# A build-time order with a model of DMA rings, single tasks held or moved, and a two-tile sum, in a DeltaNet and feed-forward kernel

## The chip, the cores and the metric

The kernel runs on one core of a Trainium2 chip. A core has TensorE (PE; its weight loads are PEld in the profile), VectorE (DVE), ScalarE (ACT), GpSimd (POOL) and SyncE (SP), which here does nothing but issue DMA transfers. Each engine works through its own list of instructions, in the order in which the program wrote them, and waits at an instruction until what it needs is there. The metric is the device time of one execution in microseconds, the median of several runs.

## The reference

Queries, keys and values are 4 x 8 x 768 x 48 in fp32 (batch, heads, time steps, width), and beta is 4 x 8 x 768. The first half is a delta rule with a 48 x 48 state for each batch and head, the second half a feed-forward layer on its result:

```python
k_n = k / (np.linalg.norm(k, axis=-1, keepdims=True) + 1e-06)
for t in range(S):
    y[:, :, t] = np.einsum('bhd,bhde->bhe', q[:, :, t], state)
    v_old = np.einsum('bhde,bhd->bhe', state, kt)
    state = state + bt[:, :, :, None] * np.einsum('bhd,bhe->bhde', kt, vt - v_old)
...
x = attn_out.transpose(0, 2, 1, 3).reshape(B * S, H * D)      # 3072 x 384
h = x @ w_in                                                  # 3072 x 2048
g = h * np.cos(h)
out = g @ w_out                                               # 3072 x 384
```

The two weight matrices come as 64-bit floats. The kernel reads them as pairs of 32-bit words and makes 32-bit floats of them on the chip.

## The kernel before, in words

**The delta rule** is done in 24 units of 32 time steps, all batches and heads at once. Inside a unit the recurrence becomes a triangular system, and only the state goes from unit to unit. Two units make a pair, and 12 pairs make the 12 token blocks (256 tokens each) of the feed-forward part. The steps of unit n, with engine and line, are these.

- Loads of k, q and v (SP, L369, four DMAs each, one for each batch; from unit 8 on k takes eight).
- The key norms: square (ACT, L495), sum (DVE, L500), square root as a power (POOL, L512), and `scale` (DVE, L523 to L531: five instructions, of which the first, L523, adds 1e-6 to the norm). For the first four units these go unit by unit, afterwards by pairs. `weigh` (DVE, L548) scales v.
- `turn` (PE transposes, L560) and `turn_out` (ACT, L570) bring k and q into the layout for the products; from unit 8 on DVE does this (L576).
- `gram` (PE, L591, 128 small matmuls) forms key by key and key by query products; `gram_keys` (DVE, L602) and `gram_queries` (DVE, L611) scale and mask them. `gram_put` (SP, L629) writes the first to DRAM. For each pair `gram_get` (SP, L638) reads them back with one system in each partition.
- `inv` is the triangular inversion of a pair, 31 steps of a product and a difference, cut into seven tasks (L667 and L674). It starts from `eye` (ACT, L648). Pair 0 is inverted on DVE (the profile's `part_v`) and copied by `inv_out` (ACT, L678); all others are inverted on POOL. `put` (SP, L683) writes the inverse to DRAM (`z_dr`), `get` (SP, L692, four DMAs a unit) reads it back transposed (`zt`).
- `state` (PE, L709), `right` (DVE, L724), `solve` (PE, L740), `solve_out` (DVE, L750), `update` (PE, L763) and its sum into the state (DVE, L771), `within` (PE, L780), `within_out` (ACT, L791), `features` (PE, L799) and `features_out` (ACT, L807), which leaves the unit's rows of x.

**The weights** come in 28 tiles: 12 of w_in (512 KB each) and 16 of w_out (384 KB each). Each has a DMA (`weights`, SP, L460), a `split` (two on ACT, L468 and L470), a `shift` (two on DVE, L474 and L479) and an `add` (POOL, L483). The 28 DMAs are chained in order, and the tiles, the gated activations and the squares share eight buffers.

**The feed-forward part** of token block p: blocks 0 and 1 multiply by w_in plainly (`hidden`, PE, L820; the name carries block and group, so hidden 08 is group 8 of block 0, and a group is one `p_h` bank of 12 matmuls), later blocks with seven products in place of eight (`layer`, L936). The gate h cos h takes ACT (L860, L872, L873) and DVE (L865, L876). The output of block 0 is plain (`out`, L962; out 001 is its second task, each of four matmuls with their weights, named block, half, part), later blocks use a seven-product scheme (L1019) with sums on DVE. The result is stored by SP (L1080).

**What sets the order.** Nothing is ordered by hand: the class `Order` is a list scheduler that runs while the program is built. Each piece of work is a task with an engine, a cost, a due time, the tasks that it needs, the buffers that it makes and uses, and, for a transfer, the DMA time that it moves. Due times go backwards from the ends. `NUDGE` then shifts them by the kind of task, with one value for early units and one for later ones. `run` simulates the engines; whenever one is free it takes the ready task with the earliest due time, and writes its instructions. Two rules bend that for TensorE. `STICK` lets it stay with small or with large tiles for tasks whose due times are near, and `stall` models the fetch of its instructions in blocks of 256. A transfer is modelled by `IN_FLIGHT`: at most eight are on their way. What the simulation is told of costs (`add(...)` in `unit`, `inverse` and `weights`) thus decides only which order comes out; the engines then run that order at their own pace, and each waits at the first instruction whose inputs or buffers are not there.

Of the kernel before, what the change touches and what calls it, by code (L numbers as in the profile page):

```python
# [11 lines left out]
FP = mybir.dt.float32  # L12
I32 = mybir.dt.int32
U32 = mybir.dt.uint32
ALU = mybir.AluOpType
# [31 lines left out]
class Order:  # L47
# [9 lines left out]
    WINDOW = 818.445  # L57
    LAG = {"PE": 0.2, "DVE": 0.15, "ACT": 0.15, "POOL": 0.2, "SP": 2.0, "IN": 0.0}
    IN_FLIGHT, ISSUE = 8, 0.49
# [3 lines left out]
    STICK = 1.823  # L63
# [22 lines left out]
    def add(  # L86
        self, key, engine, cost, emit, deps=(), makes=(), uses=(), moves=0.0, due=1e9
    ):

        assert key not in self.tasks, key  # L90
        self.tasks[key] = [engine, cost, due, emit, set(deps), makes, uses, moves]
        for t in uses:
            self.users[t] = self.users.get(t, 0) + 1
        for tag, t in makes:
            self.tiles[t] = tag

    def count(self, key):
        if key == ("state", 0):
            return 0
        if key[0] == "layer":  # L100
            return 32 if key[3] in (1, 6, 7) else 16
        return self.COUNT[key[0]]

    def stall(self, key, now, commit):

        n = count = self.count(key)

        n = int(n * 1.034 if self.written < 1000 else n * 1.0054 + self.rest)
        cost, stall, there = self.tasks[key][1], 0.0, {}
        for i in range(self.written + 1, self.written + n + 1):  # L110
            t = now + cost * (i - self.written) / n + stall
            if (i + self.PHASE + self.AHEAD) % self.BLOCK == 0:
                there[(i + self.PHASE + self.AHEAD) // self.BLOCK + 1] = t + self.FETCH
            if (i + self.PHASE) % self.BLOCK == 0:
                block = (i + self.PHASE) // self.BLOCK
                stall += max(0.0, there.get(block, self.there.get(block, 0.0)) - t)
        if commit:
            if self.written >= 1000:
                self.rest += count * 1.0054 - n
            self.written += n  # L120
            self.there.update(there)
        return stall

    def run(self, wrote):
# [16 lines left out]
        for key, task in self.tasks.items():  # L141
            n = key[1] if len(key) > 1 and isinstance(key[1], int) else 0
            if key[0] in self.PAIRED:
                n *= 2
            task[2] += self.NUDGE.get((key[0], n < self.EARLY), 0.0)
# [1333 lines left out]
```

## Time and profile before

| | |
|---|---|
| median of 3 runs | 673.85 us (673.36 to 676.03) |
| the profiled execution | 673.89 us |
| its span, first to last instruction | 672.1 us |
| TensorE busy | 612.8 us (91%) |
| TensorE weight loads busy | 573.4 us (85%) |
| VectorE, ScalarE, GpSimd busy | 476.5, 295.7, 346.5 us |
| mean granted TensorE clock | 0.992 |
| first solve starts | 59.59 us |
| inversion of pair 0 on VectorE | 27.91 to 46.02 us |
| inversion of pair 1 on GpSimd | 37.74 to 77.83 us |
| last matmul ends | 667.07 us |

The profiled execution lies within 0.04 us of the median, so its parts can be used as they stand. Its time is 1.8 us more than the span. Two stretches must be told apart: up to about 60 us TensorE has little to do and waits for the first inverse, and after about 150 us it is busy nearly all of the time. A group of the profile is a line with an engine and a shape of tile; "idle before" is the time in which that engine stood still just before such an instruction, with what released it. SPq stands for SyncE's queue of DMA issues. In an answer in order of time the first column is the start, the second the duration (for a DMA issue the time to issue the whole group), and xN the number of instructions in a row.

### The profile page before, as it was taken

Reading aid. Unit: us, or ns where it says so; the run is one execution under the profiler, and the core shown is the slowest. Engines: PE = TensorE matmul, PEld = TensorE weight load, DVE = VectorE, ACT = ScalarE, POOL = GpSimd, SP = SyncE. Lnnn points to the kernel's source line nnn. Section 1 sums busy time; section 2 is a strip of 40 time slices with the busy share of each in tenths; the row PEclk is TensorE's granted clock in tenths of the full one; section 3 lists DMA queues with packets and bytes.
Section 4 is the critical chain, followed back from the end, with each engine's and each line's share of the span. In section 5 each row is a group of like instructions: output and inputs, shape, how many; then the busy total and the mean of one; then the engine's idle time right before and its main releaser. Section 6 shows DMA issues by size and latency. Waiting matters only on the chain.

```text
span 672.1 us, 27308 instructions
## 1 busy us (share of the span) xinstructions
PE 612.8 (91%) x11864; PEld 573.4 (85%) x11864; DVE 476.5 (71%) x911; ACT 295.7 (44%) x510; POOL 346.5 (52%) x734
## 2 busy tenths in 40 slices
PE   4303798999999999999999999999999999999996
PEld 3203786896999998999999999999999999999996
DVE  5799588978676785886876876776666656656661
ACT  4432457672153543653443444444434434434530
POOL 4369878976858328586285482582481670000000
PEclk9999798999999999999999999999999999999999
DMA  8897755455463453534524524515213202000000
GB/s 180 200 207 163 171 116 154 115 98 92 70 101 63 68 87 63 101 44 69 106 39 64 110 33 66 109 25 90 52 22 60 52 6 55 1 5 24 1 24 24
DMA packets 215516, 52.56 MB, mean 78 GB/s; under 512 B 206948, under 2 KB 210164, under 8 KB 215396
## 3 DMA queue, kind: packets, MB, share of 16 engines
q1 hardware_dynamic: 212964, 49.98, 38.7%
q8 instruction: 93, 1.52, 0.9%
q10 hardware_dynamic: 2176, 0.39, 0.4%
q0 software_dynamic: 256, 0.44, 0.3%
q14 instruction: 27, 0.22, 0.1%
HBM read 39.76 MB, written 11.01 MB: 76 GB/s over the span
## 4 chain that ended last, share of the span: by engine, by line
PE 83%; SPq 4%; DMA 4%; POOL 3%; issue 2%; DVE 2%; ACT 1%; ACTq 0%; POOLq 0%
PE p_h L936 29%; PE p_out L1019 28%; PE p_h L820 5%; PE p_kq L709 4%; PE p_out L962 3%; PE p_s L763 3%; PE p_u L740 3%; PE p_kq L780 3%; PE p_g L591 2%; PE p_o L1019 2%; SPq L369 1%; PE p_z L799 1%; SPq L692 1%; POOL knrm L512 1%; DMA zt<-z_dr 1%
## 5 line engine op out<-in xcount | busy, mean ns | idle before, releaser
L667 POOL TENSOR_TENSOR part<-z,gb 128x126 f32<-128x126 f32 (+22 forms) x341 | 132.3, 388 | 108.2 <-DMA gb<-g_dr 47.0
L674 POOL TENSOR_TENSOR z<-z,part 128x126 f32<-128x126 f32 (+22 forms) x341 | 139.9, 410 | 26.7
L936 PE MATMUL p_h<-x_ffn,w_in 128*128 128x128 f32 x1120 | 143.6, 276 | 0.1
L936 PEld LDWEIGHTS p_h<-x_ffn,w_in 128*128 128x128 f32 x1120 | 135.5, 192 | 1.4 <-issue 0.2
L1019 PE MATMUL p_out<-w_out,g_ffn 128*128 128x192 f32 x672 | 123.8, 329 | 0.1
L1019 PEld LDWEIGHTS p_out<-w_out,g_ffn 128*128 128x128 f32 x672 | 107.5, 190 | 1.2
L860 ACT ACTIVATE turns<-p_h 128x512 int32<-128x512 f32 x96 | 56.9, 595 | 101.0 <-DVE p_h L955 74.6
L1019 PE MATMUL p_out<-w_sum,g_ffn 128*128 128x192 f32 x496 | 91.5, 329 | 0.0
L872 ACT ACTIVATE turns<-turns 128x512 f32<-128x512 f32 x96 | 60.4, 629 | 45.1 <-DVE turns L865 44.9
L1019 PEld LDWEIGHTS p_out<-w_sum,g_ffn 128*128 128x128 f32 x496 | 79.3, 190 | 0.9
L876 DVE TENSOR_TENSOR g_ffn<-turns,p_h 128x512 f32<-128x512 f32 x96 | 65.4, 682 | 18.8 <-ACT turns L873 18.0
L865 DVE SCALAR_TENSOR_TENSOR turns<-p_h,turns 128x512 f32<-128x512 f32 x96 | 65.5, 684 | 16.3 <-ACT turns L860 16.0
L1035 DVE TENSOR_TENSOR g_ffn<-g_ffn 128x512 f32<-128x512 f32 x88 | 62.6, 712 | 13.6 <-PE p_out L1019 13.0
L512 POOL TENSOR_TENSOR knrm<-ksum,halves 128x16 f32<-128x16 f32 (+1 forms) x14 | 36.3, 2598 | 66.8 <-DVE ksum L500 66.8
L873 ACT ACTIVATE turns<-turns,halfpi 128x512 f32<-128x512 f32 x96 | 69.3, 722 | 3.1
L955 DVE TENSOR_TENSOR p_h<-g_ffn,p_h 128x512 f32<-128x512 f32 x60 | 41.7, 695 | 38.8 <-PE p_h L936 32.8
L952 ACT COPY g_ffn<-p_h 128x512 f32<-128x512 f32 x60 | 35.0, 583 | 74.8 <-PE p_h L936 74.6
L820 PE MATMUL p_h<-x_ffn,w_in 128*128 128x128 f32 x384 | 48.3, 284 | 0.4 <-issue 0.4
L820 PEld LDWEIGHTS p_h<-x_ffn,w_in 128*128 128x128 f32 x384 | 45.7, 198 | 1.8 <-issue 0.8
L1069 DVE SCALAR_TENSOR_TENSOR o<-p_out,o 128x192 f32<-128x192 f32 x74 | 25.2, 353 | 26.3 <-PE p_out L1019 25.5
L936 PE MATMUL p_h<-x_sum,in_sum 128*128 128x128 f32 x320 | 43.7, 280 | 0.0
L936 PEld LDWEIGHTS p_h<-x_sum,in_sum 128*128 128x128 f32 x320 | 39.5, 191 | 1.1
(94 smaller groups left out, 784.9 us busy)
## 6 DMA issues: line engine op xcount, KB each, us to landing
pairs<-in_moe_w_in_dram SPq DMA_DIRECT2D x12, 512.0 KB
gb<-g_dr SPq DMA_DIRECT2D x24, 256.0 KB
pairs<-in_moe_w_out_dram SPq DMA_DIRECT2D x16, 384.0 KB
vp<-in_v_dram SPq DMA_DIRECT2D x96, 48.0 KB
out_dram<-o SPq DMA_DIRECT2D x23, 192.0 KB
z_dr<-z SPq DMA_DIRECT2D x12, 256.0 KB
zt<-z_dr SPq DMA_DIRECT2D x96, 32.0 KB
kp<-in_k_dram SPq DMA_DIRECT2D x128, 24.0 KB
```

The costliest lines, as they stand in the source:

```text
L512: nc.gpsimd.tensor_tensor(out=scales[m][2][:, part], in0=sums[m, part.start][:, 0:n], in1=halves[:, 0:n], op=ALU.pow,)
L667: eng.tensor_tensor(out=part, in0=z[:, 0:rows, j, None].to_broadcast(shape), in1=a[:, j, None, j + 1 :].to_broadcast(shape), op=ALU.mult,)
L674: eng.tensor_tensor(out=behind, in0=behind, in1=part, op=ALU.subtract)
L820: nc.tensor.matmul(p_h[:, i], w_in[:, t, (4 * k + i) * 128 : (4 * k + i + 1) * 128], xts[p][:, t, unit * 128 : (unit + 1) * 128], start=(t ...
L860: nc.scalar.activation(turns[p, f], hidden_of(p, f), AF.Copy, scale=TURN)
L865: nc.vector.scalar_tensor_tensor(out=r, in0=hidden_of(p, f), scalar=TURN, in1=t, op0=ALU.mult, op1=ALU.subtract,)
L872: nc.scalar.activation(r, r, AF.Abs)
L873: nc.scalar.activation(r, r, AF.Sin, bias=halfpi, scale=-2.0 * math.pi)
L876: nc.vector.tensor_tensor(out=place(p, f), in0=step_of(rests.pop((p, f)), f), in1=step_of(hidden_of(p, f), f), op=ALU.mult,)
L936: nc.tensor.matmul(p_h[:, e], in_sum[:, odd_tile, 4 * s + e] if a == "s" else w_in[:, a, f * 128 : (f + 1) * 128], x_sums[p][:, unit] if b ...
L1019: nc.tensor.matmul(p_o, left(p, part, a)[:, e % 4], right(e, b), start=(e == 0), stop=(e == FT // 2 - 1), skip_group_check=True,)
L1035: nc.vector.tensor_tensor(out=left(p, s, to), in0=left(p, s, one), in1=left(p, s, two), op=op)
```

## The change

No matmul, no activation and no transfer is added or left out. Four things differ.

1. **The model of transfers** in `Order.run`. The limit of eight in flight goes. In its place each queue has a ring of 128 descriptors, with a count for each kind of transfer (`DESCRIPTORS`), and an issue is held back until its descriptors fit. The model of instruction fetches gets 1.5 us more up to 130 us of model time. Some costs are closer to measured lengths: `gram_get` 1.2 to 1.0 (its transfer 1.6 to 1.8), `scale` 1.2 to 1.1, `weigh` 1.0 to 1.1 and 1.35 to 1.5, `turn` 0.9 to 1.0, `solve`, `update` and `within` of later units 0.52 to 0.66, `features` 0.35 to 0.4, the weights' transfer 1.65 to 1.8, and its factor for w_out 0.8 to 0.78, `beta_home` 0.5 to 0.8. Due times shift with `W_OUT`, `LOADS`, `FIRST`, `STEP` and a shorter `NUDGE`.
2. **Single tasks.** `HOLD` gives four tasks an earliest model time: `gram_get` of pair 1, `add` of tile 3, `gram_keys` of unit 1 and the load of v 4. `ON_ACT` gives two transfers to ScalarE's queue: `gram_put` of unit 0 and the load of weights tile 18.
3. **The 1e-6 sum.** `scale`'s first instruction becomes a sum of two tiles, with a constant tile `tiny` that one more memset fills at the start.
4. **The order that comes out.** SyncE's list up to the first fetch of an inverse, with w for a weights tile, gput, gget, put and get as above, and the four transfers of a load as one entry:

```
before: w0 k2 q2 w1 k3 q3 w2 gput0 gput1 w3 gget0 gput2 w4 gput3 k4 q4 w5 gget1 k5 v0 w6 q5 v1 w7 k6 v2 w8 put0 q6 v3 w9 get0
after:  w0 k2 q2 w1 k3 q3 w2 gput1 w3 gget0 w4 gput2 gput3 k4 w5 q4 k5 w6 v0 gget1 q5 w7 k6 v1 q6 w8 k7 put0 q7 w9 v2 get0
```

`gram_put` of unit 0 stands in ScalarE's list behind the square of unit 2's keys, and weights tile 18 behind `features_out` of unit 1.

TensorE's list from the first solve on:

```
before: solve0 update0 within0 gram4 state1 features0 solve1 hidden00 turn5 hidden02 update1 within1 hidden04 gram5 state2 hidden06 features1 out000 solve2 hidden08 update2 within2 hidden010 hidden012 features2 state3 turn6 out001 solve3
after:  solve0 update0 within0 features0 state1 gram4 hidden00 solve1 hidden02 turn5 hidden04 update1 within1 gram5 state2 features1 out000 turn6 hidden06 hidden08 solve2 hidden010 update2 within2 hidden012 features2 out001 gram6 state3
```

On VectorE the shift of tile 1 and the sum of unit 3's squares move ahead of `gram_keys` of unit 1, the shift of tile 2 ahead of `gram_keys` of unit 2, and the shift of tile 3 ahead of the first inversion. On GpSimd the add of tile 1 moves ahead of the norms of unit 3, and adds of w_in and w_out stand between the parts of the inversion of pair 1 in another order. From there to the end the lists of both kernels are alike but for neighbours that change places; TensorE changes between small and large tiles 166 times in place of 172.

The core of the diff (the costs listed above are left out of it, and the old `NUDGE`, which had a value for nearly every kind of task):

```diff
@@ class Order: constants @@
-    WINDOW = 818.445
+    WINDOW = 832.069
     LAG = {"PE": 0.2, "DVE": 0.15, "ACT": 0.15, "POOL": 0.2, "SP": 2.0, "IN": 0.0}
-    IN_FLIGHT, ISSUE = 8, 0.49
+    RING, ISSUE = 128, 0.49
+    DESCRIPTORS = {
+        "weights": 8, "gram_put": 64, "gram_get": 4, "put": 128, "blocks": 32, "store": 8,
+        "store_left": 8, "store_right": 8,
+    }
...
-    STICK = 1.823
+    STICK = 1.267
...
+    EARLY, NUDGE = 6, {('features', False): -50.6, ('left', True): 40.0, ('solve', True): -42.0, ('turn', False): 18.7, ('within', True): -6.1, ('weigh', False): -47.8, ('within', False): -19.2, ('features', True): -15.5, ('gate', True): -31.7, ('layer_out', False): -12.4, ('sum', False): 24.3, ('layer', False): -1.8, ('add', True): -16.7, ('update', False): -6.1, ('solve', False): -32.9, ('state', False): -9.6, ('right', True): 34.9, ('hidden', True): 14.3, ('gram', False): -8.1, ('out', True): -13.0, ('collect', True): -13.1, ('out', False): 0.3, ('x_sum', False): -20.0, ('inv', True): 1.1, ('v', True): 15.4, ('gram_put', False): 23.6, ('left', False): 26.9}
+    ON_ACT = {('gram_put', 0): 1, ('weights', 18): 1}
+    HOLD = {('gram_get', 1): 35.16, ('add', 3): 48.72, ('gram_keys', 1): 18.48, ('v', 4): 72.13}
@@ Order.add @@
+        if key in self.ON_ACT:
+            assert moves
+            engine = "ACT"
@@ Order.descriptors, new @@
+    def descriptors(self, key):
+        n = self.DESCRIPTORS.get(key[0], 16)
+        if key[0] in ("k", "gram_put") and key[1] >= 8:
+            n //= 2
+        return n
@@ Order.stall @@
-                there[(i + self.PHASE + self.AHEAD) // self.BLOCK + 1] = t + self.FETCH
+                there[(i + self.PHASE + self.AHEAD) // self.BLOCK + 1] = (
+                    t + self.FETCH + (1.5 if t < self.STEADY else 0.0)
+                )
@@ Order.run @@
-            task[2] += self.NUDGE.get((key[0], n < self.EARLY), 0.0)
+            task[2] += self.NUDGE.get((key[0], n < self.EARLY), 0.0) + self.NUDGE.get(key, 0.0)
...
-        flights, dma_free, hot = [5.5] * 4 + [8.5] * 4, 8.0, 1e9
+        flights, accepted, hot = [(7.0, 8.0, 8, "SP")], {}, 1e9
...
-                able = [x for x in heap if x[0] <= limit and fits(x[2])]
+                able = [
+                    x for x in heap
+                    if x[0] <= limit and fits(x[2]) and self.HOLD.get(x[2], 0.0) <= now
+                ]
...
                     for _ in range(parts):
-                        end = max(end, flights[-self.IN_FLIGHT]) + self.ISSUE
-                        dma_free = max(dma_free, end + 0.5) + moves / parts
-                        flights.append(dma_free + 1.4)
-                    done = flights[-1]
+                        end = max(end, accepted.get(engine, 0.0))
+                        begin = max(flights[-1][1], end + 0.95)
+                        flights.append(
+                            (begin, begin + moves / parts, self.descriptors(key), engine)
+                        )
+                        accepted[engine], room = end + 0.3, self.RING
+                        for a, b, n, on in reversed(flights):
+                            if on != engine:
+                                continue
+                            if n > room:
+                                accepted[engine] = max(
+                                    accepted[engine], a + (b - a) * (n - room) / n
+                                )
+                                break
+                            room -= n
+                        end += self.ISSUE
+                    done = flights[-1][1] + 1.4
@@ the kernel @@
+    def queue(*key):
+        return nc.scalar if key in Order.ON_ACT else nc.sync
...
+    tiny = const.tile([128, 2, H], FP, name="tiny")
+    nc.vector.memset(tiny, 1e-6)
...
-        nc.sync.dma_start(out=words[t], in_=src)
+        queue("weights", t).dma_start(out=words[t], in_=src)
...
-        nc.vector.tensor_scalar_add(knrm, knrm, 1e-6)
+        nc.vector.tensor_tensor(out=knrm, in0=knrm, in1=tiny[:, 0:n], op=ALU.add)
...
-            nc.sync.dma_start(
+            queue("gram_put", n).dma_start(
                 out=g_dr[heads, bs].rearrange("h b j i -> (b j) h i"), in_=g[rows, heads]
             )
@@ the tasks @@
-    W_IN, W_OUT, LOADS = 24.824, 4.888, 290.255
+    W_IN, W_OUT, LOADS = 24.824, -43.991, 290.993
...
-    FIRST, STEP = 2.12, 3.854
+    FIRST, STEP = 2.668, 3.87
```

## The prediction

> **What bounds the kernel now.** I read the busy times by stretch first, then TensorE's waits, then the SP queue and VectorE in order of time. The stretches (columns after the length: PE, PEld, DVE, ACT, POOL busy with counts, granted clock, DMA share, GB/s):
>
> ```profile
> 0.00:59.60 59.60, 14.26 (x297) 11.48 (x298) 46.29 (x127) 21.82 (x39) 33.81 (x52) 1.00 0.88 191
> 59.60:79.40 19.80, 15.07 (x445) 13.30 (x446) 11.73 (x26) 6.87 (x13) 17.61 (x35) 0.83 0.70 157
> 79.40:150.60 71.20, 68.18 (x1394) 59.70 (x1393) 60.13 (x102) 47.32 (x89) 58.30 (x85) 0.98 0.55 127
> 150.60:672.10 521.50, 515.25 (x9733) 488.86 (x9731) 358.30 (x659) 219.71 (x372) 236.76 (x564) 1.00 0.32 56
> ```
>
> From 150.6 on TensorE is busy 515.25 of 521.5 us, and some 5 of the rest is the tail after the last matmul (667.07). The same work must be done after the change, so only the first 150 us can move the end. TensorE's waits (total, times, longest):
>
> ```profile
> PE p_u L740 <- DMA zt<-z_dr: 25.6, 3, 25.0
> ...
> PE p_kq L709 <- issue: 2.5, 1, 2.5
> ...
> PE p_t L560 <- issue: 1.5, 1, 1.5
> ```
>
> The 25 us is the first solve, which starts at 59.59. I call that moment S. Behind it lies this chain: gram_keys, put and gather through DRAM, first inversion on VectorE (27.91 to 46.02), copy on ScalarE (to 46.69), then SP's queue:
>
> ```profile
> 47.22 0.71 SPq L460 DMA_DIRECT2D pairs<-in_moe_w_in_dram  x1
> 48.03 0.39 SPq L683 DMA_DIRECT2D z_dr<-z  x1
> 48.51 4.25 SPq L369 DMA_DIRECT2D qp<-in_q_dram  x4
> 52.80 1.94 SPq L369 DMA_DIRECT2D vp<-in_v_dram  x4
> 54.83 0.39 SPq L460 DMA_DIRECT2D pairs<-in_moe_w_in_dram  x1
> 55.27 4.23 SPq L692 DMA_DIRECT2D zt<-z_dr  x8
> ```
>
> The inverse is ready at 46.69, but SP reaches its put at 48.03: the queue, at 0.49 us an issue, ends last. The first of the four issues behind the put takes 2.77 us alone, where others take 0.45[...]. Later, TensorE loses time here:
>
> ```profile
> 107.26 1.38 PE L709 MATMUL p_kq<-st,kq_t 48*32 48x48 f32 x128
> 109.49 0.66 PE L560 MATMUL p_t<-consts,kp 128*128 128x128 f32 x4 [0.86 <-ACT x_ffn L807]
> 111.64 0.66 PE L560 MATMUL p_t<-consts,qp 128*128 128x128 f32 x4 [1.49 <-issue]
> 112.14 4.44 PE L962 MATMUL p_out<-w_out,g_ffn 128*128 128x384 f32 x8
> ```
>
> Eight output matmuls take 4.44 us here and 2.75 elsewhere: 1.7 us lost to the clock, after 2.35 us of gaps.
>
> [...] 93 instruction packets of 16 KB on queue 8, and all three "issue" gaps (ending 70.61, 75.84, 111.64) stand at one position modulo 256 in TensorE's stream; from 70.61, when one block arrives, to 75.84, when the next does, are 5.2 us. [...] the hidden group at 74.04 takes 5.3 us, later ones 2.84. [...] L523 took 1.25 us instead of 0.17 when L483 had begun 0.06 us before it, L474 1.76 instead of 0.68. [...]
>
> **The change, part by part.**
>
> *A. Up to the first inversion.* The 1e-6 sum is the same instruction count. [...] the edit alone is worth 0; the bound is 1.08 us saved at the fourth scale (1.25 less 0.17) and 0.1 lost. But POOL's second add now stands before the fourth norm, so nothing on POOL reads beside that scale: 1.08 is won by order. Against it, VectorE gets the fourth shift (0.68 + 0.43, 1.0 with overlap) ahead of the inversion, not behind it. And gram_keys of unit 1 moves behind the second shift and the fourth sum: second split ends 17.04, shift 1.0 (2.3 if POOL's add at 17.60 blocks it), sum 0.54, keys 0.41: done at 19.1 to 20.4, not 16.81. Its put goes out at 19.2 to 20.5. From second put to gather it was 4.5 us (18.50 to 22.99) behind two puts and one weights tile; one put less is about 1.2, so gather at 22.5 to 23.8, and 4.9 more (22.99 to 27.91): 27.4 to 28.7. VectorE itself: fourth scale at 22.5, 1.0; two shifts 2.0; four gram products 1.65: 27.2. So the inversion starts near 28.0, as before (27.91).
>
> *B. The SP queue to the z put.* From the third weights tile (done 17.88) SP had 46 issues to the put; it now has 49 (one g put goes to ScalarE; two loads of four move ahead of it, k 7 and q 6, one behind it, v 2). Before: 22.5 us of issue, 7.6 of waiting (30.15 in all). The waiting now: 1.9 for gram_keys 1 (was 0.2); 0 at the fourth weights tile (its 2.00 us lost 1.55 behind two puts); 2.3 at the gather (1.8); about 2.2 where two g puts follow the gather and a weights tile directly, with k 4 behind them (1.5); 2.4 over the rest, as before. 24.0 + 8.8: the put at 50.7, 2.6 later. The inverse, ready at 46.7, no longer matters.
>
> *C. Put to solve.* 11.56 us before (48.03 to 59.59), and again nine issues between put and fetch. The weights tile now stands before v, not right before the fetch: some 0.4 less. S' = 50.7 + 11.2 = 61.9, 2.3 later.
>
> *D. S' to the first hidden group and second solve.* Before, S + 19.8 with gram 4, state 1, features 0, solve 1 and hidden. Now features 0 comes first and waits for ScalarE's copy (0.46 and its hand-over) until +7.1; 0.77; state 1, 2.4: +10.3. [...] a 2 us stall, where it was 2.54. Gram 1.1, hidden 5.3, solve 1.5: +20.2. Loss 0.4; if the fetch runs ahead of that wait, a gain of 1.3.
>
> *E. Weights and POOL.* Gram 4 now ends at S' + 13.3 = 75.2 (66.97 before). SP stands at its put until 75.8, and behind that put wait the next weights tile (13), v 4 and tile 14. Tile 13 lands 3.6 later, split 1.0, its shift behind solve_out: its add ends at 85. POOL's order holds one more add (1.4), the last quarter of inversion 1 (5.3) and two adds (2.0) before the first output: 93.9; then three adds (4.1): 98. TensorE from 82.1: hidden 2.85, turn 1.0, hidden 2.9, update 0.9, within 0.9, gram 0.8, state 1.35, features 0.5: 93.3. The output waits 0.6 and takes 2.75, turn 1.1: 97.8; two hidden groups of 2.9 from 98: 103.8. Before, that set (turn 6 for solve 2) stood at 100.1. So +3.7 in all at this point.
>
> *F. Given back.* Turn 6 no longer stands behind state 3, and before state 3 now come output and gram, so that block has 4.6 us and more: the 2.35 us of gaps and the 1.7 of clock should go: -4.05. TensorE changes between small and large tiles 166 times, not 172; 2.94 against 2.84 for the same hidden group puts a change at 0.1: -0.6.
>
> *G. Other orders.* The new due times shuffle neighbours to the end of the run, mostly by one or two places; the same matmuls, with TensorE as cover. The weights tile issued from ScalarE waits for a free buffer on ScalarE; its activations queue behind it, covered by several us. What the cover misses I put at +1.5, from 0 to 4.
>
> Sum: 3.7 - 4.05 - 0.6 + 1.5 = +0.6 on 673.89 (the profiled execution: span 672.1 and 1.8 around it; it agrees with the median, 673.85). That is 674.5.
>
> **The rivals.**
> 1. *Slower, through E.* The late z put and SP's stand at gram 4's put push weights and adds so late that TensorE waits longer for L483 than F gives back. For: POOL is busy 58 of 71 us in that stretch, and add 11 came just in time before. Against: filler exists. It decides once the adds slip some 3 us beyond 98. With S' 1.5 later, 3 more there and 1 us of half clock: 680.
> 2. *Faster.* The put isn't late: the waits at loads shrink with the smaller queue, put at 48.2, S' 59.4, D's fetch ahead. Then -0.2 - 1.3 + 0.5 - 4.05 - 0.6: about 668.3. Against: 49 issues cost 24.0 us by themselves.
> 3. *Nothing of it reaches the end*, because TensorE has other work: that is the forecast's band.
>
> **Numbers.** 0.5% is 3.4 us, about what a measurement of this kernel tells from no change. Forecast band (670.5 to 677.3): 0.47. Slower: 0.32. Faster: 0.21. Range 668 to 681: A to E each carry about 1.2 us, F up to 4.
>
> **What would show it.** z put near 50.7 and first solve near 62: B and C. First output's wait for L483: E. No gap near turn 6 and 2.75 us for the second output group: F. The fourth scale at 1.0 us: A. It would be wrong if SP's waits before the put fell below 6 us, or a new gap of over 3 us came anywhere after 104.

## The result, and the profile after

The changed kernel takes 674.52 us (median of 12 runs, 672.76 to 677.73), beside 673.85 us for the kernel before (12 runs, 672.44 to 677.87). The ratio is 1.0006, with a 95% interval from 0.9989 to 1.0023: no difference that a measurement of this kernel can tell. The forecast was 674.5 us, with a band of 670.5 to 677.3 us for no difference.

The profiled execution of the changed kernel took 676.72 us (span 674.9), 2.2 us over its median. Single executions of one program are several microseconds apart here (those of the kernel before lie between 668.70 and 678.89 us over all the comparisons below). One pair of traces therefore shows where time goes, but not to a microsecond what the change is worth. A place is trusted below when several traces with the same order show it. Line numbers of the changed kernel are 39 higher than before at the loads of q, k and v (L369 is now L408) and 41 higher from the loads of weights on (L740 is now L781). The profile lists each fp32 matmul of the program as two records, so a hidden group of twelve stands as x24, an output task of four as x8, and a gram product, which has 32 matmuls and not 128, as x64.

Busy times by stretch of the changed kernel, cut at its first solve, at the end of its first hidden group and where the fourth output task of block 0 ends (columns as before: length, busy time and count of PE, PEld, DVE, ACT, POOL, granted clock, DMA share, GB/s):

```profile
0.00:60.30 60.30, 14.44 (x296) 11.46 (x297) 45.70 (x132) 23.51 (x41) 29.86 (x45) 1.00 0.87 190
60.30:77.30 17.00, 13.79 (x383) 12.21 (x386) 9.88 (x21) 4.33 (x8) 15.28 (x27) 0.80 0.64 156
77.30:149.50 72.20, 68.54 (x1460) 60.18 (x1460) 60.48 (x104) 47.64 (x88) 63.03 (x100) 1.00 0.58 130
149.50:674.90 525.40, 515.72 (x9732) 490.33 (x9730) 359.41 (x658) 218.79 (x373) 240.02 (x564) 1.00 0.32 55
```

The last stretch holds the same work as before (515.72 us of TensorE beside 515.25) and is 3.9 us longer. The cut at 149.50 comes 1.1 us earlier than its counterpart, 150.60. TensorE's waits (total, times, longest):

```profile
PE p_u L781 <- DMA zt<-z_dr: 23.4, 2, 22.8
...
PE p_kq L750 <- issue: 4.3, 4, 1.6
...
PE p_h L861 <- POOL w_in L524: 1.0, 1, 1.0
```

The wait for the first inverse is still the longest. The waits for instructions at the state product grew from 2.5 us in one place to 4.3 us in four, and the longest other new wait behind the first solve is one of 1.0 us for an add of w_in on GpSimd. SyncE's queue from the put of the inverse to its fetch:

```profile
50.87 0.40 SPq L724 DMA_DIRECT2D z_dr<-z  x1
51.37 3.45 SPq L408 DMA_DIRECT2D qp<-in_q_dram  x4
54.91 0.39 SPq L501 DMA_DIRECT2D pairs<-in_moe_w_in_dram  x1
55.35 1.91 SPq L408 DMA_DIRECT2D vp<-in_v_dram  x4
57.31 1.93 SPq L733 DMA_DIRECT2D zt<-z_dr  x4
```

The put goes out at 50.87, 2.84 us later than before, the fetch at 57.31, 2.04 later, and the first solve starts at 60.32, only 0.73 later. TensorE in the first hidden group after the first output (hidden 06, two matmuls in; the line runs on through hidden 08), at the second output task, and at the state product of unit 5:

```profile
96.54 5.18 PE L861 MATMUL p_h<-x_ffn,w_in 128*128 128x128 f32 x44 [1.01 <-POOL w_in L524]
...
111.14 0.49 PE L840 MATMUL p_z<-consts,y 128*128 128x128 f32 x3
111.46 2.75 PE L1003 MATMUL p_out<-w_out,g_ffn 128*128 128x384 f32 x8
...
171.45 0.74 PE L750 MATMUL p_kq<-st,kq_t 48*32 48x48 f32 x56 [1.58 <-issue]
172.12 4.55 PE L1060 MATMUL p_out<-w_out,g_ffn 128*128 128x192 f32 x16
```

The place around 110 us, where the kernel before lost 2.35 us in gaps and 1.7 to the clock (granted 0.62 from 112.1 to 116.6 us), is clean (granted 1.00 from 111.5 to 114.3). A new one stands at 170: a stop of 1.58 us in the middle of the state product, and behind it sixteen records in 4.55 us, for which the next sixteen need 2.87 (the granted clock was 0.62 from 172.1 to 176.6 us, 1.00 before and after). A second stop, 1.48 us, is at 312.5.

### The profile page after: what moved, and what is told of

Same layout as the page of the kernel before. It is cut to its first block, busy times and chain, and to the rows that moved or that the text cites. A ratio compares the mean times of both kernels' runs of the same rounds, so it can differ in the third digit from the quotient of the medians.

```text
span 674.9 us, 27292 instructions
## 1 busy us (share of the span) xinstructions
PE 612.5 (91%) x11864; PEld 574.2 (85%) x11864; DVE 475.5 (70%) x912; ACT 294.3 (44%) x510; POOL 348.2 (52%) x734
## 4 chain that ended last, share of the span: by engine, by line
PE 83%; DMA 8%; POOL 4%; issue 2%; ACT 1%; DVE 1%; SPq 1%; POOLq 0%; ACTq 0%
PE p_h L977 29%; PE p_out L1060 29%; PE p_h L861 5%; PE p_kq L750 4%; DMA pairs<-in_moe_w_in_dram 3%; PE p_out L1003 3%; PE p_s L804 3%; PE p_u L781 2%; PE p_kq L821 2%; PE p_g L632 2%; PE p_o L1060 2%; POOL part L708 1%; POOL z L715 1%; DMA z_dr<-z 1%; PE p_z L840 1%
## 5 line engine op out<-in xcount | busy, mean ns | idle before, releaser
L708 POOL TENSOR_TENSOR part<-z,gb 128x126 f32<-128x126 f32 (+22 forms) x341 | 137.6, 404 | 100.1 <-DMA gb<-g_dr 44.0
L1060 PEld LDWEIGHTS p_out<-w_out,g_ffn 128*128 128x128 f32 x672 | 109.3, 192 | 2.1 <-issue 0.5
```

What stands on the lines that cost most here:

```text
L708: eng.tensor_tensor(out=part, in0=z[:, 0:rows, j, None].to_broadcast(shape), in1=a[:, j, None, j + 1 :].to_broadcast(shape), op=ALU.mult,)
L1060: nc.tensor.matmul(p_o, left(p, part, a)[:, e % 4], right(e, b), start=(e == 0), stop=(e == FT // 2 - 1), skip_group_check=True,)
```

## The experiments

Two questions followed. Are the new stops at 170 and 312 us what takes back the start's gain? And does the time of the first solve, with which the sum began, reach the end at all? In all the kernels below but the eighth, the scheduler is replaced by a fixed list of its tasks (the list that it wrote itself, with the edit shown), so that one engine's order can be edited and the others stay. (Where a task of another engine must move with it, the edit shows that too.) "Before" and "after" name the two kernels; the ratios are to the kernel before.

### 1 and 2. The new start with the old rest, and the reverse

```diff
 the list of tasks of every engine, cut behind output task 011 (about 153 us):
-  after ... | after ...
+  after ... | before ...     # the first kernel
+  before ... | after ...     # the second
```

> The changed kernel up to the second task of block 0's second output half (about 153 us), and from there every engine in the order of the kernel before. First theory: the new start gains 1.2 us by 150 us, and the new order behind it gives this back in two places where TensorE waits for its instructions in the middle of a state product (1.59 us at 169.9, with 1.7 us of half clock behind it, and 1.48 us at 312.5). Then this kernel has no such wait after 150 us and takes 672.6 us, 1.2 under the kernel before. Second theory: the start is what costs, the two waits belong to one execution, and the order of the rest is worth nothing: 674.5 us, as the changed kernel.

> The complement: the kernel before up to the same task, and from there the order of the changed kernel. First theory: both waits at the state products are there again, at about 171 and 314 us, and the time is 2 to 3.6 us over the kernel before, 676 to 677.5 us. Second theory: 673.9 us, as the kernel before.

The new start with the old rest took 675.67 us (ratio 1.0024, 1.0002 to 1.0045). The old start with the new rest took 673.45 us (1.0000, 0.9980 to 1.0020). The second one's trace has the stop again, at the state product of unit 5:

```profile
171.54 0.73 PE L709 MATMUL p_kq<-st,kq_t 48*32 48x48 f32 x55 [1.12 <-issue]
172.20 2.87 PE L1019 MATMUL p_out<-w_out,g_ffn 128*128 128x192 f32 x16
```

It has one at 310.7 us too, of 0.63 us. So the stops belong to the order and not to one execution, but they are shorter here (1.75 us together, not 3.06), and no half clock follows. The whole kernel is not slower for them. The first theory falls: it wanted 672.6 us for the first kernel and 676 to 677.5 for the second. In the first kernel's trace the old rest loses about as much in other places (0.50 us at 174.6, 0.74 in two stops near 246, 0.70 at 283.5). The new rest is worth nothing that these runs can tell. If either half costs something, it is the new start, by 1.6 us (0.1 to 3.0 by the interval), though the changed kernel, with the same start, is not measurably slower.

The start's gain, too, is found in one trace only. The fourth output task of block 0 ends at 149.5 us in the changed kernel, where the kernel before has 150.7. But it ends at 151.3 and 151.6 in the traces of kernels 1 and 3, which have the same start, and at 150.0 in kernel 2, which has the old one.

### 3. The state products moved away from the gram products

```diff
 TensorE, unit 5:
-  gram8 state5 out110 out111 solve5 out120
+  gram8 out110 out111 state5 out120 solve5
 TensorE, unit 11:
-  gram14 state11 out351 features10 layer417 solve11
+  gram14 out351 features10 layer417 state11 solve11
 VectorE:
-  turn_out9 right5
+  right5 turn_out9
```

> The changed kernel with two tasks moved on TensorE: the state product of unit 5 behind the next two output products (and its solve behind one more), and that of unit 11 behind an output product, the features and a layer step, so that no state product follows a gram product directly in these two places. First theory: the waits of 1.59 and 1.48 us go, with the half clock behind the first; 2 to 4 us less than the changed kernel, 671 to 672.5 us. Second theory: the time stays at 674.5 us, whether the waits are in the trace or not.

Measured: 681.33 us, ratio 1.0114 (1.0092 to 1.0136), the slowest of all. The trace shows what came instead of the two stops:

```profile
178.19 2.32 PE L1060 MATMUL p_out<-w_sum,g_ffn 128*128 128x192 f32 x8 [2.88 <-DVE o L1110]
...
320.65 0.59 PE L781 MATMUL p_u<-rhs,zt 32*32 32x48 f32 x40 [0.69 <-issue]
322.24 0.54 PE L781 MATMUL p_u<-rhs,zt 32*32 32x48 f32 x24 [1.00 <-issue]
```

At 178 the output product out 120 waits 2.88 us for VectorE to collect an earlier one. On VectorE that collecting stands behind `right` of unit 5, which needs the state product, and this now comes later. At 322 the stop for instructions (1.00 us) is back, 256 instructions further on, in the solve behind the state product. The 0.69 us at 320 stand at another place in a block, and their cause is open. Both theories miss: with the stops taken away at their places the kernel takes 6.8 us more than the changed one.

### 4. An earlier first solve: the put moved ahead

```diff
 SyncE:
-  q6 w8 k7 put0 q7 w9 v2 get0 w10 get1
+  q6 put0 w8 k7 q7 get0 w9 v2 w10 get1
```

> The changed kernel with SyncE's put of the first inverse moved ahead of weights tile 8 and the loads of k 7, and the first fetch of it moved ahead of weights tile 9 and v 2. The put goes out at 48.4 us (50.87 in the changed kernel), the first solve starts near 58.2 (60.32). If the adds on GpSimd decide how much of this arrives, the wait for L524 before the second hidden group after the first output grows from 1.0 to 3 us, and the whole time stays within 0.7 us of the changed kernel. If TensorE alone sets the pace up to 104 us, as the sum of the prediction had it for a change of the first solve, the time is 2 us less, 672.5 us.

The put went out at 48.80 and the first solve started at 57.29, 3.0 us earlier than in the changed kernel. The time was 675.6 us, ratio 1.0015 (0.9998 to 1.0032): not less.

```profile
64.87 1.56 PE L804 MATMUL p_s<-u,kp 64*64 64x96 f32 x32 [4.78 <-DVE knrm L564]
```

The gain is gone after one step. The first update waits 4.78 us and starts at 64.87, where the changed kernel has 63.80. It needs the scaled solution from VectorE, and there that stands behind the shift of tile 9, which comes late now:

```profile
62.54 0.69 DVE L515 SCALAR_TENSOR_TENSOR pairs<-pairs 128x512 uint32<-128x512 uint32 x1 [1.25 <-ACT pairs L511]
63.15 0.64 DVE L520 TENSOR_SCALAR w_in<-w_in 128x512 uint32<-128x512 uint32 x1
63.71 1.01 DVE L791 TENSOR_TENSOR u<-p_u,bz 128x384 f32<-128x384 f32 x2
```

The fetch was moved ahead of the load of tile 9, so the tile's split and shift are later, and VectorE goes through its list in order. (The view names L564, the short instruction right behind the scaled solution.) Neither expectation had named VectorE.

### 5. Step F alone, in the kernel before

```diff
 TensorE:
-  out000 solve2 hidden08 update2 within2 hidden010 hidden012 features2 state3 turn6 out001 solve3 hidden014
+  out000 turn6 hidden08 solve2 hidden010 update2 within2 hidden012 features2 state3 hidden014 out001 solve3
 ScalarE:
-  split17 cos06 ... split20 turn_out6
+  turn_out6 split17 cos06 ... split20
```

> The kernel before, with step F alone: on TensorE the transposes of unit 6 go ahead of hidden 08, hidden 10 behind the second unit's solve, and hidden 014 between the state product of unit 3 and the second output. If F was right by itself, the gaps of 0.86 and 1.49 us at 108.6 and 110.2 us go, the output behind them takes 2.75 us, and the end comes 2.3 us earlier, 4 with the half clock. The rival: the second output waits for an add of w_out on GpSimd (L483, done at 112.31 in the kernel before) whatever stands ahead of it, TensorE only waits elsewhere, and the whole time is within 1 us of the kernel before.

Measured: 673.81 us, ratio 0.9998 (0.9979 to 1.0016). The rival is right about the time and in that TensorE waits elsewhere. Its reason, the add on GpSimd, is not seen: the second output starts at 115.13 without a wait. The gaps around the transposes are gone, and others stand in their place:

```profile
110.51 0.28 PE L709 MATMUL p_kq<-st,kq_t 48*32 48x48 f32 x5 [1.78 <-issue]
110.72 4.57 PE L820 MATMUL p_h<-x_ffn,w_in 128*128 128x128 f32 x24
115.13 2.75 PE L962 MATMUL p_out<-w_out,g_ffn 128*128 128x384 f32 x8
...
119.92 0.85 PE L591 MATMUL p_g<-kq_t 48*32 48x64 f32 x64 [1.23 <-DVE u L750]
```

The stop for instructions moves from the transposes into the state product (1.78 us), the loss of speed falls on the hidden group (4.57 us for what takes 2.94), and the next gram product waits 1.23 us for VectorE.

### 6. The gather of pair 1 early again

```diff
 SyncE:
-  k4 w5 q4 k5 w6 v0 gget1 q5
+  k4 w5 gget1 q4 k5 w6 v0 q5
```

> The changed kernel with the gather for the inversion of pair 1 issued behind weights tile 5 instead of behind v 0, which undoes what the hold on it did. The inversion on GpSimd starts near 37.5 us (43.30), and the adds behind it come some 5 us earlier up to 90 us. If GpSimd sets the pace between 90 and 104 us, as step E had it, the wait of 1.0 us for the last w_in add at 95.5 goes and the end comes 1 us earlier. If TensorE has other reasons, nothing moves at 104 us but the wait.

The inversion on GpSimd started at 38.9 us, as meant. The time was 676.68 us, ratio 1.0043 (1.0022 to 1.0065). It is slower, and neither expectation had that. The put of the first inverse went out at 53.09 and the first solve started at 63.02, 2.7 us later. GpSimd, ahead at first, then waited for tiles (from 74.9 to 77.6 and from 81.1 to 83.5), had the second inverse ready at 92.1 instead of 90.4, and TensorE waited for that:

```profile
105.22 0.24 PE L781 MATMUL p_u<-rhs,zt 32*32 32x48 f32 x2 [1.52 <-DMA zt<-z_dr]
105.94 0.49 PE L781 MATMUL p_u<-rhs,zt 32*32 32x48 f32 x4 [0.48 <-DMA zt<-z_dr]
106.71 0.86 PE L781 MATMUL p_u<-rhs,zt 32*32 32x48 f32 x58 [0.29 <-DMA zt<-z_dr]
107.51 4.57 PE L861 MATMUL p_h<-x_ffn,w_in 128*128 128x128 f32 x24
```

So holding this one gather is worth about 2.5 us inside the new order (1.0043 beside 1.0006; the two intervals touch), though the inversion behind it begins 4.4 us later for it.

### 7. Everything early

```diff
 SyncE:
-  k4 w5 q4 k5 w6 v0 gget1 ... v1 q6 w8 k7 put0 q7 w9 v2 get0 w10 get1 v3
+  k4 w5 gget1 q4 k5 w6 v0 ... v1 w8 put0 q6 k7 get0 get1 w9 v2 v3 q7 w10
 VectorE:
-  in_sums30 shift9 solve_out0 scale(pair 2) shift10 update_out0 weigh1
+  solve_out0 in_sums30 update_out0 scale(pair 2) weigh1 shift9 shift10
 ScalarE:
-  split8 square(pair 3)
+  square(pair 3) split8
```

> The early gather, and with it the put of the first inverse ahead of q 6, its fetches ahead of weights tile 9, v 2, v 3 and q 7; on VectorE the first scaling of a solution ahead of the shift of tile 9, and that shift behind the second pair's weighing. Put at 47.6 us, first solve near 57.5, first update at 60.8 (63.80 in the changed kernel). If the first solve, the copy of its solution and GpSimd's adds together carry the start, TensorE is 3 us ahead at 104 us and the whole time is 3 us under the changed kernel, 671.5 us. If something else stands in between, its name will be at the longest new wait between 60 and 104 us.

First solve at 57.51 as expected, and 677.78 us, ratio 1.0058 (1.0040 to 1.0075).

```profile
63.14 1.56 PE L804 MATMUL p_s<-u,kp 64*64 64x96 f32 x32 [3.30 <-DVE u L791]
...
72.25 0.90 PE L840 MATMUL p_z<-consts,y 128*128 128x128 f32 x3 [6.12 <-ACT y L832]
```

The new wait has a name: 6.12 us for the copy of y on ScalarE (L832). ScalarE's order in time, same kernel:

```profile
63.90 0.67 ACT L509 ACTIVATE w_in<-pairs 128x512 f32<-128x512 f32 x1 [4.75 <-DMA pairs<-in_moe_w_in_dram]
...
70.62 0.66 ACT L509 ACTIVATE w_in<-pairs 128x512 f32<-128x512 f32 x1 [5.51 <-DMA pairs<-in_moe_w_in_dram]
71.19 0.64 ACT L511 ACTIVATE pairs<-pairs 128x512 uint32<-128x512 uint32 x1
71.73 0.46 ACT L832 COPY y<-p_kq 128x384 f32<-128x384 f32 x1
```

The copy stands behind the splits of tiles 9 and 10. Both wait for their tiles, 4.75 and 5.51 us, because those loads had been moved back.

### 8. The two-tile sum alone, in the kernel before

```diff
-        nc.vector.tensor_scalar_add(knrm, knrm, 1e-6)
+        nc.vector.tensor_tensor(out=knrm, in0=knrm, in1=tiny[:, 0:n], op=ALU.add)
```

> The kernel before with the 1e-6 sum as a sum of two tiles and nothing else. In the kernel before the fourth of these sums took 1.25 us with an add on GpSimd at work, others 0.17. If both forms wait for GpSimd alike, it takes 1.1 to 1.3 us here too. If the two-tile form runs freely beside it, 0.17, and the inversion starts up to 1 us earlier unless the gather from DRAM ends last.

One execution, 670.67 us, which decides nothing on the time. The sum itself is clear, VectorE first and GpSimd below:

```profile
22.23 1.24 DVE L525 TENSOR_TENSOR knrm<-knrm,tiny 128x8 f32<-128x8 f32 x1 [1.19 <-POOL knrm L514]
```
```profile
22.17 1.28 POOL L485 TENSOR_TENSOR w_in<-w_in,pairs 128x512 uint32<-128x512 uint32 x1
```

1.24 us beside an add on GpSimd that began 0.06 us earlier, exactly what the one-tile form took there. The third sum took 1.25 us beside another such add; the first two took 0.17 us, where GpSimd did nothing. In the changed kernel, where the add stands elsewhere, the fourth sum takes 0.17. The edit by itself shortens nothing here, and the order is what frees the sum, as step A had it.

### 9. A later put

```diff
 SyncE:
-  k7 put0 q7 w9 v2 get0
+  k7 q7 put0 w9 v2 get0
```

> The changed kernel with SyncE's put of the first inverse behind the load of q 7 instead of ahead of it: the put near 52.8 us (50.87), its fetch when it has landed, the first solve near 62.8 us (60.32). This is step B and C with the sign that the prediction gave them. If a later first solve goes through to the end, the time is 2 to 2.5 us over the changed kernel, some 0.4% over the kernel before. If the work behind it (adds, copies on ScalarE, VectorE) gives TensorE cover, as it did for an earlier solve, the time is within 0.7 us of the changed kernel.

```profile
53.89 0.40 SPq L724 DMA_DIRECT2D z_dr<-z  x1
...
57.65 2.29 SPq L733 DMA_DIRECT2D zt<-z_dr  x4
```

The put is 3.0 us later than in the changed kernel, but the fetch leaves at 57.65, just 0.34 later, and the first solve starts at 60.98, 0.66 later. 674.76 us, ratio 1.0010 (0.9994 to 1.0026). The put has landed within 3.8 us. In this trace the issues ahead of the fetch set it, and it hardly matters on which side of the put they stand. The expectation of 62.8 us for the solve was wrong, and the time within 0.7 us right.

### 10. The start arranged again

```diff
 SyncE:
-  k4 w5 q4 k5 w6 v0 gget1 ... v1 q6 w8 k7 put0 q7 w9 v2 get0 w10 get1 v3
+  k4 w5 gget1 q4 k5 w6 v0 ... v1 w8 put0 w9 q6 k7 get0 get1 w10 v2 v3 q7
 ScalarE:
-  split8 square(pair 3) split9 split10 within_out0 split11 features_out0
+  split8 split9 square(pair 3) within_out0 features_out0 split10 split11
 VectorE:
-  sum(pair 3) beta_home in_sums30 shift9 solve_out0 scale(pair 2) shift10 update_out0 weigh1
+  beta_home solve_out0 in_sums30 update_out0 shift9 scale(pair 2) sum(pair 3) weigh1 shift10
 GpSimd:
-  add12 add7 add8 add13 add9 inv16 add14 add15 add16 add10 add11
+  add7 add8 add9 inv16 add12 add13 add10 add11 add14 add15 add16
```

> The start of the changed kernel arranged again with every wait that the earlier first solve met taken out of its way: SyncE issues the gather for pair 1 behind weights tile 5, the put of the first inverse behind tile 8, tile 9 right behind it, then q 6, k 7 and the fetches; ScalarE makes the split of tile 10 behind the first copy of features; VectorE makes the first scaled solution ahead of the shift of tile 9; GpSimd adds tiles 7 to 11 ahead of those of w_out. First solve near 57.5 us (60.32), first update near 61 (63.80), state product of unit 1 near 65 (67.86). If the chain from the first solve is what the first 100 us wait for, the end comes 2.5 to 3 us earlier than in the changed kernel, 671.5 us. If the instruction blocks take it back (the gap ahead of the product of unit 4 grows from 0.64 to 3 us), or the weight tiles do, the whole time stays within 1 us of the changed kernel.

The start goes as meant: first solve 57.49, first update 61.27, state product 65.69, first hidden group 69.05 (71.90 in the changed kernel). But the time is 677.6 us, ratio 1.0060 (1.0036 to 1.0084; the trace is of the fastest of its five runs, 674.01 us).

```profile
85.19 0.89 PE L804 MATMUL p_s<-u,kp 64*64 64x96 f32 x32 [1.46 <-ACT kq_t L611]
...
89.70 0.80 PE L632 MATMUL p_g<-kq_t 48*32 48x64 f32 x60 [2.80 <-DVE st L812]
...
93.06 5.25 PE L1003 MATMUL p_out<-w_out,g_ffn 128*128 128x384 f32 x8
```

TensorE's lead of 2.85 us at 69 is gone by 93 us, where the first output now starts 3 us after that of the changed kernel (90.09): VectorE and ScalarE, whose work was pushed behind the first solve, are late around the second one.

### 11. The weights tile away from the fetch, in the kernel before

```diff
 SyncE:
-  put0 q6 v3 w9 get0 get1
+  put0 q6 w9 v3 get0 get1
```

> The kernel before with one thing moved on SyncE: weights tile 9 goes ahead of the load of v 3 and so no longer stands right before the fetch of the first inverse. The fetch is issued at the same time (55.27 to 56.26 in four traces of this start). If a 512 KB tile right ahead is what made the way from fetch to first solve 4.07 to 4.32 us there, it is 3.0 to 3.4 us here, as in the changed kernel, where four loads stand between, and the first solve starts near 58.7 us. If the length belongs to something else in the old start, it stays at 4.1 to 4.3. In either case the whole time stays within 0.7 us of the kernel before, since an earlier first solve met other waits in three runs.

```profile
53.71 0.39 SPq L460 DMA_DIRECT2D pairs<-in_moe_w_in_dram  x1
54.15 1.91 SPq L369 DMA_DIRECT2D vp<-in_v_dram  x4
56.10 4.83 SPq L692 DMA_DIRECT2D zt<-z_dr  x8
```

First solve at 59.83, so 3.73 us from fetch to solve. That lies between the two forecasts: in this one execution the tile explains about half of the difference. 675.48 us, ratio 1.0021 (0.9994 to 1.0049).

### 12. The first gram put back on SyncE

```diff
-    ON_ACT = {('gram_put', 0): 1, ('weights', 18): 1}
+    ON_ACT = {('weights', 18): 1}
 SyncE:
-  w2 gput1 w3
+  w2 gput0 gput1 w3
```

> The changed kernel with the first put of gram products back on SyncE, ahead of the second, as in the kernel before; weights tile 18 stays on ScalarE. If issuing it elsewhere saved the time of one issue alone, SyncE reaches the fetch of the first inverse 0.4 to 0.5 us later (57.3 to 57.8 in the traces of this start), and the whole time does not change beyond 0.7 us. If the put on its own queue also kept the others short, the gather of pair 0 and the fetch come 1 us or more later.

```profile
31.50 0.40 SPq L501 DMA_DIRECT2D pairs<-in_moe_w_in_dram  x1
...
52.67 0.41 SPq L724 DMA_DIRECT2D z_dr<-z  x1
...
57.47 2.74 SPq L408 DMA_DIRECT2D vp<-in_v_dram  x4
60.25 1.94 SPq L733 DMA_DIRECT2D zt<-z_dr  x4
```

The fetch left at 60.25, 2.5 to 2.9 us later than in the three traces with this start unaltered (57.31, 57.78, 57.41), more than the one issue accounts for. The gather of pair 0 did not move (22.90 beside 22.76 to 23.02), and SyncE came to weights tile 5 at 31.50, inside the range of those three traces (30.90 to 31.67). The time was lost after that, in loads that SyncE issued more slowly up to the fetch (the last four ahead of it took 2.74 us instead of 1.91). The delay of the fetch is thus seen in one execution, and how the put would cause it is not shown. And yet the time is 673.89 us, ratio 1.0002 (0.9983 to 1.0022).

## Why the prediction was right

The time was right, and so was the forecast that the difference would be too small to measure. The sign says nothing: +0.6 us was forecast and +0.7 measured, well inside the noise. Neither of the two signs of being wrong came: SyncE's waits before the put are 8.9 us by the count of step B, and the longest new gap after 104 us is 1.58 us. Of the steps some were right and some wrong, and the runs show that the first of them do not carry the result. That the number came so close is luck.

**A, up to the first inversion.** The value of the edit alone (nothing) was the author's estimate, and the eighth kernel shows it; of the two examples that the prediction gave, L474 is another operation (scalar_tensor_tensor), and kernel 8 shows the sum of two tiles itself. The fourth scale took 1.02 us, as said. gram_keys of unit 1 at 19.42, its put at 20.32 and the gather at 22.76 lie in the ranges given. The inversion started at 29.00, not 28.0; in the other traces with this start at 28.75 to 29.47, with the old one at 27.52 to 28.98. The gather took longer to land than the 4.9 us taken from before. Nothing waits for it: the inverse is ready at about 47.7, and SyncE reaches its put at 50.87.

**B, SyncE's queue.** Right: 50.7 said, 50.87 measured (51.36 and 51.03 in the other two traces).

**C, put to solve.** Wrong by 1.7 us: 11.2 said, 9.45 measured. The failing term is "some 0.4 less": it is about right for the weights tile that no longer stands right before the fetch, but it was taken for all that changes between put and solve. From fetch to solve it was 4.07 to 4.32 us in four traces with the tile right ahead, 3.01 to 3.37 with four loads between, 2.01 to 2.48 with the tile six or more microseconds ahead. Kernels 9 and 12, where the tile stands 3.3 and 3.5 us ahead with four loads between, have 3.33 and 2.41. The eleventh kernel, which moves the tile alone, gives 3.73: so the tile is worth 0.3 to 0.6 us by itself. What makes up the rest, no run takes apart. Besides, the first issue of loads behind the put held the queue for 1.97 us, not 2.77.

**D, to the fourth gram product.** Said S + 13.3, measured S + 11.65. The stop for instructions was 0.64 us, not 2. The 2 was the author's estimate, from the 5.2 us between the ends of two stops before. Those 5.2 us are no constant: in the kernel before, whole blocks of 256 instructions are worked off in 2.98 us (at 168.2) and in 1.87 us (at 190.0) without a stop behind them.

**E, weights and GpSimd.** The mechanism is there in the hidden group behind the first output (1.01 us of waiting for L524 at 96.54); the 0.6 us at that output itself did not come, and the size is not as said. First output at 90.09, not 93.9; hidden 08 done at 101.72, not 103.8. Against the step's own comparison, 100.1 before, the kernel is 1.6 us later there, not 3.7, and C's and D's misses, 3.2 us together at the end of the fourth gram product, more than account for the difference. A further 1.4 us went in the solve behind it, which takes 2.27 us instead of 0.88 (0.54 of it waiting for its fetched inverse). No step had that.

**F, given back.** The place is clean and the output takes 2.75 us, as said. From the end of the second pair's solve to the end of the second output, this pair of traces has 10.29 us after and 14.34 before for the same work (one hidden group, the transposes and the state product, which are elsewhere after, taken out): 4.05 us, as said. As the value of an order it was wrong. The old start was without the 1.7 us of half clock by itself in the second kernel (2.75 us for the same output), and step F done alone gained nothing (the fifth).

**G, the rest.** +1.5 said (0 to 4). In the pair of traces it is more, 3.9 us after the fourth output task, by two stops and the half clock behind one. Over many runs the new rest costs 0.0 us (0.9980 to 1.0020 with the old start). The 0.6 us for fewer changes of tile were not tried. And the opening of the prediction, that only the first 150 us can move the end, is wrong: kernel 3 changes the order behind 165 us alone and takes 6.8 us more than the changed kernel.

**The sum.** By the steps, the first solve's delay went 1:1 into the end until something gave it back. This is the assumption that the runs take away. Four kernels with the changed kernel's order on TensorE, and with the gather of pair 1 held, differ in the first solve by 5.4 us and in nothing that can be measured at the end:

| kernel | put | fetch | first solve | ratio to before |
|---|---|---|---|---|
| 4, put first | 48.80 | 55.28 | 57.29 | 1.0015 (0.9998 to 1.0032) |
| the changed kernel | 50.87 | 57.31 | 60.32 | 1.0006 (0.9989 to 1.0023) |
| 9, put later | 53.89 | 57.65 | 60.98 | 1.0010 (0.9994 to 1.0026) |
| 12, put on SyncE | 52.67 | 60.25 | 62.66 | 1.0002 (0.9983 to 1.0022) |

Passed on 1:1, the ratio of kernel 4 would lie 0.0045 below that of the changed kernel and that of kernel 12 0.0035 above it; they lie 0.0009 above and 0.0004 below. An earlier solve meets VectorE (kernel 4), ScalarE (7) or both at the second unit (10). Where a later one is made good is not shown. In kernel 12 the wait for the w_in add at about 98 us is 0.72 us instead of 1.01, and the first output takes 2.75 us, not 3.25; but against the changed kernel's trace the delay is still 2.4 us at the fourth output task (151.9 beside 149.5), and against those of kernels 1 and 3 (151.3 and 151.6) little of it is left. The third rival, "nothing of it reaches the end, because TensorE has other work", describes the result better than the sum that gave the number, though it is not TensorE alone that has the other work. In the pair of traces the terms are about +3.0, -4.0 and +3.9; over many runs the last is nothing, and step F, tried alone, gains nothing. The number came out right because terms of opposite sign, too large for what the runs show, nearly cancelled.

What stays open: why the early gather of pair 1 costs 2 to 3 us. It is common to kernels 6, 7 and 10, three of the four slowest, but was changed alone in kernel 6 only, and the later second inverse seen there was not tested by itself. Nor was the load of weights tile 18 on ScalarE tried alone. No version here was faster than both kernels.

## What to carry to other kernels

Where several in-order engines are each busy most of a stretch, the longest wait of the bottleneck engine is not worth its length: before pricing an earlier release, walk to the next instruction of each engine that must answer it and ask what stands ahead of that one in its list. Moving work out of a stop's way moved the stop (kernels 3 and 5); price the place where it goes as carefully as the one that it leaves. And when single executions are several microseconds apart, take a place as real only when it recurs in traces with the same order.

## What the runs showed of the hardware

- The stop for instructions on TensorE follows the position in its stream. With the new order unchanged there, one stands in the state product of unit 5 in all eight traces: 1.58 us in the changed kernel, and 1.12, 1.29, 1.56, 1.61, 1.12, 1.04 and 1.39 in kernels 2, 4, 6, 7, 9, 10 and 12. The trace has 93 instruction packets of 16 KB on queue 8 beside 11,864 matmul records and as many weight loads, 255 of these to a packet. In the stream of TensorE the stop of 1.58 us stands 15 times 256 instructions behind the place where the kernel before stops for 2.54 us. Counted in instructions, the block before the stop was entered at about 168.2 us and ran out at 169.87. A packet on queue 8 began at 168.52 and took 1.49 us, and TensorE went on at 171.45, some 3.2 us after the entry. A short block does not always stop TensorE: the one of 1.87 us named under D has no stop behind it.
- Half clock came behind this stop in the changed kernel's own trace alone: sixteen records took 4.55 us there (granted clock 0.62 from 172.1 to 176.6 us) and 2.87 in all the seven others, at the same place of the same order. A stop of 1.0 to 1.6 us is thus followed by it in one trace of eight.
- Beside an add on GpSimd that took 1.28 us and began 0.06 us earlier, a sum of two tiles on VectorE (128 x 8) took 1.24 us in kernel 8, and 0.17 where GpSimd did nothing. The one-tile form took 1.24 us beside the same add in the kernel before (1.27 us, begun 0.07 us earlier).
- Behind the put of the first inverse, the next issue of a load took SyncE 2.77 us in the kernel before and 1.97 in the changed one, where others take 0.45. No run here shows that a put moved to ScalarE's queue saves SyncE more than its own issue: the 2.5 to 2.9 us of kernel 12 are one execution, and arise more than 10 us behind the put.
